# Preparing q and k of a head two heads ahead instead of one, with a third buffer for the transposed operands

## The chip, the cores and the metric

The kernel runs on one core of one Trainium2 chip. Its time is the device time of one launch in microseconds (us). Before the change the median of three runs is 1237.27 us (1229.78, 1237.27 and 1239.12).

## The reference: what is computed

Eight batches of eight heads, 576 positions, 64 columns a head. Attention with a bias from a running sum, then a gated feed-forward layer (FFN) on the 4608 x 512 result:

```
scores = q @ k.T / 8 + min(-(cum[i] - cum[j]), 0)      cum = cumsum(max(s, 0))
scores = where(j > i, -1e9, scores)
attn   = exp(scores - rowmax);  attn /= rowsum + 1e-9
x      = heads side by side of (attn @ v)               4608 x 512
out    = (sigmoid(x @ w_gate) * (x @ w_val)) @ w_out    d_ff = 1536
```

## The kernel before

**The arithmetic.** From head 8 on, float32 operands are split into a high and a low float16 part, and a product is made of several float16 matmuls. For q and k this takes four steps, in `split_qk` and `swap_k`. ScalarE (ACT) writes the high parts of q and k (L370, L372), VectorE (DVE) the low parts (L371, L373), into a tile `t16` of 96 x 12 x 2 x 64. A transposing DMA (L375) issued by SyncE (SP) turns that into `T[i][:, 0:2]`, with the columns of a head down the partitions. Two plain DMAs (L380, L381), also from SP, then write into `T[i][:, 2]` a copy of k's part in which the upper and the lower 64 partitions have changed places. SP issues L380 only once the transposition has landed.

**The scores.** A head has 576 rows in five row tiles (64 rows, then four times 128), worked from the last, t = 4, to the first. For each, `s_part` makes the scores on TensorE (PE) in two matmuls into the same bank: L420 with `T[i][:, 0]`, which needs the transposition alone, and L421 with `T[i][:, 2]`, which needs the two swapping DMAs. Row tile 4 is done in two pieces of 288 columns, so a head has six L420 and six L421. The banks are three ("s", "s", "x"). DVE adds the bias row and takes the row minimum (`max_part`, L445), which frees the bank; POOL masks the bias row (L435); ACT makes the exponential (L448).

**The weights and the output of attention.** `p_part` splits the exponentials (ACT L452, DVE L453), and SP transposes them by DMA (L456, tile `pt`, two a head). `av_part` multiplies them with v on PE (L468 to L470) two heads later.

**The FFN.** A unit (`ffn_in`, L615) is 24 or more matmuls of one group of 256 tokens and one of twelve columns of d_ff into a bank pair `gv`, of which there are two. ACT takes the tanh (L620), DVE the product (L622), which frees the pair. ACT and DVE split the product (L630, L631), and `ffn_out` multiplies with `w_out` (L645).

**What sets the order.** One loop over ticks, five ticks a head (`NTL = 5`), emits a piece of everything: the scores of one row tile, masks and minima of the tile before, the output of an earlier head, the preparation of a later head at fixed ticks, and so many FFN units that a batch's units are spread over the ticks of the next batch. A scheduler takes this emission order as the priority and arranges each engine's instructions with its own estimates of when operands will be there. At run time each engine works off its own list strictly in order and waits where something is missing. Instructions inside `pin(...)` keep the order of the program among themselves.

**The stages.** Heads 0 to 7 use another form (`n_prep`, `n_s`). From tick 90 (head 18, `NOFF + 3`) the space of `t2big`, used before for the first FFN units, becomes free: `more_room` takes a second buffer for `t16` (`qk16`) and one for the loaded q and k (`qk32`) out of it. In profiles and orders those two appear under the name `t2f`. Up to there they have one buffer each. `T` has two buffers of a pool throughout, so `T[i]` is written over `T[i-2]`.

**When q and k are prepared, from head 18 on.** Heads go in pairs p = i // 2, with j = i % 2; all times are ticks t of head i. In an even head (j = 0) the other head of the pair is split at t = 1 and swapped at t = 3. In an odd head (j = 1) the next pair is squared at t = 0 (ACT L340 and a reduction on POOL, for a power of two that scales it), scaled at t = 1 (DVE L348 to L358), the first head of it is split at t = 2 and swapped at t = 4. Its first scores are emitted at the tick that follows.

Of the kernel before, what the change touches and what calls it, by code (L numbers as in the profile page):

```python
# [7 lines left out]
F16 = mybir.dt.float16  # L8
# [8 lines left out]
P = 128  # L17
# [6 lines left out]
def tile_attention_then_gated_ffn(  # L24
# [12 lines left out]
    B, H, S, D = q.shape  # L37
# [166 lines left out]

    def more_room():
        c = 0
        for name, n in (("qk16", QC * 2 * D), ("qk32", 4 * QC * D)):
            spare[name] = t2big[:, c : c + n]
            c += n

# [150 lines left out]
    def split_qk(i):  # L361
        p, j = divmod(i, 2)
        sc = qkc[p][0]
        if spare and i % 2:
            t16 = spare["qk16"][:QP].bitcast(F16).rearrange("p (a c l d) -> p a c l d", a=2, l=2, d=D)
        else:
            t16 = wp.tile([QP, 2, QC, 2, D], F16, tag="qk16", name=f"qk16_{i}", bufs=1)
        q_ = qk32[p][:, 0, j]
        k_ = qk32[p][:, 1, j]
        pin(nc.scalar.activation(t16[:, 1, :, 0], q_, AF.Copy, scale=sc[:QP, 0:1]))  # L370
        nc.vector.scalar_tensor_tensor(t16[:, 1, :, 1], q_, sc[:QP, 0:1], t16[:, 1, :, 0], ALU.mult, ALU.subtract)  # L371
        nc.scalar.activation(t16[:, 0, :, 0], k_, AF.Copy, scale=sc[:QP, 1:2])  # L372
        nc.vector.scalar_tensor_tensor(t16[:, 0, :, 1], k_, sc[:QP, 1:2], t16[:, 0, :, 0], ALU.mult, ALU.subtract)  # L373
        T[i] = wp.tile([P, 3, S], F16, tag="T", name=f"T{i}", bufs=2)
        nc.sync.dma_start_transpose(  # L375
            T[i][:, 0:2].rearrange("p a (c n) -> p (a c) n", n=QP),
            t16.rearrange("p a c l d -> p (a c l d)"))
# [302 lines left out]

    NE, NOFF = 44, 87
    FPT = 1.5
    WLA = 3
    nticks = NTL * NH
    for n in range(nticks + 12):
        if n == NOFF + 3:
# [36 lines left out]

        if t == 1 and NN <= i - 2 < NH:
            with first(NE <= n < NOFF):
                av_part(i - 2, 1)
                av_part(i - 2, 0)
                x_part(i - 2)
            if i % 2 == 1:
                split_x((i - 2) // 2)  # L730

        if i < NH:
            p, j = divmod(i, 2)
            b, h = divmod(i, H)
            if t == 0 and i + 1 < NH:
                load_crow(i + 1)
            if t == (2 if spare else 0) and i + 1 < NH:
                spread_crow(i + 1)
            if i + 2 < NN:
                if j == 0 and t == 1:  # L740
                    n_load(p + 1)
                    load_v(p + 1)
                if j == 1 and t == 2:
                    with first():
                        n_prep(p + 1)
            elif j == 0 and i + 2 < NH:
                if t == 2:
                    if p + 1 not in qk32:
                        load_qk(p + 1)
                    load_v(p + 1)  # L750
                if t == 4 and not spare:
                    qk_square(p + 1)
            if NN <= i and j == 0:
                if t == 0:
                    split_v(p)
                if t == 1:
                    split_qk(i + 1)
            if NN - 1 <= i and j == 1 and i + 1 < NH:
                late = 1 if spare else 0
                if t == 0 and p + 1 not in qkc:  # L760
                    qk_square(p + 1)
                if t == late:
                    qk_scale(p + 1)
                if t == 1 + late:
                    split_qk(i + 1)
                if t == 3 and spare and i + 3 < NH:
                    load_qk(p + 2)
            if t == (3 + j if spare else 3) and NN - 1 <= i and i + 1 < NH:
                swap_k(i + 1)
            if b == 0:  # L770
                if 1 <= n < 1 + vch:
                    v_square(0, n - 1)
                if n == 1 + vch:
                    v_scale(0)
            if b + 1 < B:
                if t == 2 and 1 <= h < 1 + vch:
                    v_square(b + 1, h - 1)
                if t == 4 and 1 <= h < 1 + vch:
                    v_square_sum(b + 1, h - 1)
                if t == 1 and h == 6:  # L780
                    v_scale(b + 1)
            while n < NE and wnext["step"] < min(2 + n // 8, 6):
                weight_step()

        if n >= NE and state["u"] < 2 * NF:
            fdone = min(NF, int((n - NE + 1) * FPT))
            while state["u"] < 2 * fdone:
                f = state["u"]
                if f < NF and f % WLA == 0:
                    while wnext["step"] < f + WLA:  # L790
                        weight_step()
                    inverse_weights(0, slice(f, f + WLA))
                    ffn_scale(0, slice(f, f + WLA))
                while f >= NF and wnext["step"] < min(f + NF + WLA, len(wsteps)):
                    weight_step()
                emit_unit()
            if state["u"] == 2 * NF:
                hidden_scale()
                while state["o"] < 2 * NF:
                    emit_out()  # L800
                late_slots()
        if (n - 30) % (NTL * H) == 0 and n >= 30 + NTL * H:
            ffn_scale((n - 30) // (NTL * H))
        m = n - (9 if n > 2 * NTL * H + 30 else 7)
        b = m // (NTL * H) if m >= 0 else 0
        if b >= 1:
            r = m - b * NTL * H + 1
            done = min(NT, b * S) // GT * NF if b < B else len(units)
            prev = min(NT, (b - 1) * S) // GT * NF
            want = prev + (done - prev) * r // (NTL * H)  # L810
            while state["u"] < min(want, len(units)):
                emit_unit()
# [32 lines left out]
```

## Time and profile before

| | |
|---|---|
| median of three runs | 1237.27 us |
| the profiled execution: its own time / its span | 1237.8 us / 1236.0 us |
| mean granted clock of PE | 0.971 |
| PE busy | 1121.7 us, 91% |
| DVE / ACT / POOL busy | 785.8 us (64%) / 747.1 us (60%) / 302.9 us (25%) |
| scores of heads 8 to 63 on PE, lines L420 and L421 | 111.9 to 1055.5 us of the span |

A group's row gives the line, the engine, the operation, output and inputs, the number of instructions, then busy time, the mean duration of one in ns and the idle time of the engine just before them with what ended it. A row of waits reads: engine, tile and line that waited, what it waited for, the total in us, how many times, the longest. In a timeline each row starts with the start and the duration in us; a bracket at the end gives the idle time before it and what ended it. `SPq` is SyncE issuing a DMA: its duration is the issuing, not the transfer. A row of windows gives for each engine the busy time and the instructions in it, then the granted clock of PE, the share of the DMA engines that is busy and what they moved. After 1055 us there is only the FFN of the last batch.

### The profile page before, as it was taken

The page shows a single profiled execution, that of the slowest core. Times are in us where ns is not written, and L with a number is a line of the kernel's source. Part 1 is how long each engine was busy: PE and PEld are TensorE (multiplying, and loading weights), DVE is VectorE, ACT ScalarE, POOL GpSimd, SP SyncE. Part 2 cuts the span into 40 slices and gives each one's busy share as a digit, 9 for nine tenths or more (in the row PEclk, how much of TensorE's full clock was granted, in tenths as well). Part 3 has the DMA queues.
Part 4 walks back from the last instruction along what each step waited for, and adds up shares of the span by engine and source line. Part 5 has one row for each costly group of instructions (what it writes and reads, how often), then busy time and mean ns, then how long its engine had stood idle before and what let it go on. Part 6 is the DMA issues. An engine that isn't in the chain of part 4 may idle for free.

```text
span 1236.0 us, 30675 instructions
## 1 busy us (share of the span) xinstructions
PE 1121.7 (91%) x11924; PEld 870.4 (70%) x11924; DVE 785.8 (64%) x2194; ACT 747.1 (60%) x1505; POOL 302.9 (25%) x605
## 2 busy tenths in 40 slices
PE   6787789899998899889999989998899899999997
PEld 5575568567776777577777766777777777787774
DVE  6899898767776677556656667765677677322221
ACT  6998786766666666455655656665576666333221
POOL 5544343222132222221212122322232311000000
PEclk9888899999999899899999999999999999999999
DMA  9665897967779777975546576677777755200000
GB/s 276 196 191 120 202 200 153 164 145 148 143 141 153 120 159 144 135 141 92 120 82 138 118 151 138 128 135 148 132 150 144 130 105 122 54 19 7 12 18 18
DMA packets 464176, 157.51 MB, mean 127 GB/s; under 512 B 438495, under 2 KB 457951, under 8 KB 464030
## 3 DMA queue, kind: packets, MB, share of 16 engines
q1 hardware_dynamic: 446302, 119.89, 52.5%
q0 software_dynamic: 5440, 18.88, 5.0%
q10 hardware_dynamic: 12288, 16.78, 4.3%
q8 instruction: 93, 1.52, 0.6%
q14 instruction: 53, 0.43, 0.1%
HBM read 56.92 MB, written 9.58 MB: 54 GB/s over the span
## 4 chain that ended last, share of the span: by engine, by line
PE 38%; issue 22%; DMA 16%; DVE 10%; ACT 6%; SPq 3%; POOL 2%; ACTq 0%; POOLq 0%; DVEq 0%
PE gv L615 20%; PE o L645 10%; DMA T<-T 8%; DMA T<-qk 6%; PE s L421 3%; DVE e L445 2%; PE s L420 2%; SPq L456 1%; SPq L380 1%; DVE p L453 1%; PE av L470 1%; PE av L468 1%; PE av L469 1%; ACT p L452 1%; ACT w L276 1%
## 5 line engine op out<-in xcount | busy, mean ns | idle before, releaser
L615 PE MATMUL gv<-x,w 128*128 128x256 f16 (+3 forms) x6912 | 635.0, 248 | 4.0 <-DVE t2f L622 4.0
L615 PEld LDWEIGHTS <-w 128*128 128x128 f16 x6912 | 541.5, 99 | 72.3 <-issue 5.8
L645 PE MATMUL o<-w2all,h 128*128 128x512 f16 x1296 | 320.0, 383 | 0.0
L435 POOL TENSOR_SCALAR_AFFINE_SELECT rl<-rl 128x64 f32<-128x64 f32 (+1 forms) x280 | 131.3, 471 | 491.1 <-DVE em L445 394.0
L620 ACT ACTIVATE th<-gv,scb 128x256 f32<-128x256 f32 (+3 forms) x288 | 111.5, 413 | 216.6 <-PE gv L615 215.4
L448 ACT ACTIVATE e<-e,em 128x576 f32<-128x576 f32 x280 | 153.8, 555 | 112.9 <-DVE em L445 111.7
L445 DVE CUSTOM_DVE_ANT_0 e<-s,rl,qkcf 128x288 f32<-128x288 f32 x280 | 136.1, 486 | 110.9 <-PE s L421 99.0
L645 PEld LDWEIGHTS <-h 128*128 128x128 f16 x1296 | 124.1, 99 | 106.7 <-issue 3.8
L622 DVE SCALAR_TENSOR_TENSOR t<-th,gv 128x256 f32<-128x256 f32 x192 | 80.2, 418 | 162.5 <-ACT th L620 161.7
L453 DVE SCALAR_TENSOR_TENSOR p<-e,p 128x1152 f16<-128x1152 f32 x112 | 129.6, 1157 | 39.5 <-ACT p L452 39.4
L630 ACT ACTIVATE h<-t,hsc 128x256 f16<-128x256 f32 x192 | 96.9, 505 | 75.7 <-DVE t L622 75.6
L631 DVE SCALAR_TENSOR_TENSOR h<-t,hsc,h 128x256 f16<-128x256 f32 x192 | 93.5, 487 | 53.6 <-ACT h L630 53.0
L421 PE MATMUL s<-T 128*128 128x288 f16 x336 | 81.2, 288 | 48.1 <-DMA T<-T 48.1
L452 ACT ACTIVATE p<-e 128x1152 f16<-128x1152 f32 x112 | 111.4, 994 | 1.2
L420 PE MATMUL s<-T 128*128 128x288 f16 x336 | 82.4, 280 | 24.4 <-DMA T<-qk 19.5
L468 PE MATMUL av<-v,pt 128*128 128x65 f16 x840 | 88.8, 193 | 4.3 <-DMA pt<-p 4.1
L469 PE MATMUL av<-v,pt 128*128 128x64 f16 x840 | 88.6, 193 | 0.0
L470 PE MATMUL av<-v,pt 128*128 128x65 f16 x840 | 88.4, 195 | 0.0
L468 PEld LDWEIGHTS <-pt 128*128 128x128 f16 x840 | 77.9, 98 | 12.2 <-DMA pt<-p 5.5
L469 PEld LDWEIGHTS <-pt 128*128 128x128 f16 x840 | 77.7, 97 | 7.0 <-issue 0.2
L421 PEld LDWEIGHTS <-T 128*128 128x128 f16 x336 | 30.7, 100 | 71.7 <-DMA T<-T 53.3
L470 PEld LDWEIGHTS <-pt 128*128 128x128 f16 x840 | 77.7, 97 | 2.4 <-issue 0.2
(165 smaller groups left out, 1228.4 us busy)
## 6 DMA issues: line engine op xcount, KB each, us to landing
vsq<-in_v_dram POOLq DMA_DIRECT2D x32, 288.0 KB, 4.5
out_dram<-osb POOLq DMA_DIRECT2D x36, 256.0 KB, 2.6
v<-in_v_dram SPq DMA_DIRECT2D x64, 128.0 KB
T<-T SPq DMA_DIRECT2D x112, 72.0 KB
ws<-in_moe_w_out_dram ACTq DMA_DIRECT2D x12, 512.0 KB
qk<-in_q_dram SPq DMA_DIRECT2D x17, 288.0 KB
qk<-in_k_dram SPq DMA_DIRECT2D x17, 288.0 KB
w2all<-in_moe_w_gate_dram ACTq DMA_DIRECT2D x7, 512.0 KB
```

The source lines that it names most:

```text
L421: nc.tensor.matmul(ps[:, : b_ - a], lhs, T[i][:, 2, a:b_], start=False, stop=True)
L435: nc.gpsimd.affine_select(rl[i][:, q0:w], rl[i][:, q0:w], pattern=[[-1, m]], compare_op=ALU.is_ge, fill=-MASKED if i < NN else MASKED, bas ...
L445: nc.vector.tensor_tensor_reduce(e_t[t][:, a:b_], ps[:, : b_ - a], rl[i][:, a:b_], c, init, ALU.add, ALU.min, acc)
L448: nc.scalar.activation(e_t[t][:, :w], e_t[t][:, :w], AF.Exp, bias=init, scale=-1.0)
L452: nc.scalar.activation(p_s[h_][:, 0], e_s[h_], AF.Copy, scale=PSCALE)
L453: nc.vector.scalar_tensor_tensor(p_s[h_][:, 1], e_s[h_], PSCALE, p_s[h_][:, 0], ALU.mult, ALU.subtract)
L468: nc.tensor.matmul(AV[i][:, t], hi, v_[:, D : 2 * D + 1], start=kb == 0, stop=False)
L469: nc.tensor.matmul(AV[i][:, t, 0:D], hi, v_[:, 0:D], start=False, stop=False)
L470: nc.tensor.matmul(AV[i][:, t], lo, v_[:, D : 2 * D + 1], start=False, stop=kb == t)
L615: nc.tensor.matmul(ps[:, gv, a:e], w1[f][:, cc, gv, wl], x_of(b, cc)[:, xl, c0 + a : c0 + e], start=(c == 0), stop=(c == 3 * NC - 1))
L620: nc.scalar.activation(th[:, a:e], ps[:, 0, a:e], AF.Tanh, scale=scb[b][:, f : f + 1])
L645: nc.tensor.matmul(ps[:m], h[:, hl, tt * P : tt * P + m], w2[f][:, wl], start=(f == 0 and c == 0), stop=(f == NF - 1 and c == 2))
```

## The change

From tick 90 the preparation runs two heads ahead. In an even head i the next pair is squared at t = 0, scaled at t = 1, its first head i + 2 is split at t = 2 and swapped at t = 4. In an odd head i, head i + 2, the second of that pair, is split at t = 1 and swapped at t = 3. `load_qk` moves with it: in an odd head, at t = 3, it loads pair p + 3 instead of p + 2. Since three heads' transposed operands are now alive, `T` gets a third buffer out of `t2big`, which every third head (i % 3 == 2) takes; the others share the two of the pool. `T[i]` is thus written over `T[i-3]`. Heads 18 to 20 are a passage: head 19 still prepares head 20, and splits head 21 as well at t = 4. What is computed, and how many instructions of each kind, stays the same. `EARLY = 18` names the head; `NTL * EARLY` is 90 as `NOFF + 3` was.

```diff
     def more_room():
         c = 0
-        for name, n in (("qk16", QC * 2 * D), ("qk32", 4 * QC * D)):
+        for name, n in (("qk16", QC * 2 * D), ("qk32", 4 * QC * D), ("T", 3 * S // 2)):
             spare[name] = t2big[:, c : c + n]
...
-        T[i] = wp.tile([P, 3, S], F16, tag="T", name=f"T{i}", bufs=2)
+        if spare and i % 3 == 2:
+            T[i] = spare["T"].bitcast(F16).rearrange("p (a n) -> p a n", a=3)
+        else:
+            T[i] = wp.tile([P, 3, S], F16, tag="T", name=f"T{i}", bufs=2)
...
+            elif i <= EARLY + 1:
+                if j == 0:
+                    if t == 1:
+                        split_qk(i + 1)
+                    if t == 3:
+                        swap_k(i + 1)
+                        load_qk(p + 2)
+                else:
...
+                    if t == 2:
+                        split_qk(i + 1)
+                    if t == 4:
+                        swap_k(i + 1)
+                        split_qk(i + 2)
+                        load_qk(p + 3)
             elif j == 0 and i + 2 < NH:
+                if t == 0:
+                    if i == EARLY + 2:
+                        swap_k(i + 1)
+                    qk_square(p + 1)
+                if t == 1:
+                    qk_scale(p + 1)
                 if t == 2:
-                    if p + 1 not in qk32:
-                        load_qk(p + 1)
-                    load_v(p + 1)
...
+                    split_qk(i + 2)
+                if t == 4:
+                    swap_k(i + 2)
+            elif j == 1 and i + 2 < NH:
                 if t == 1:
-                    split_qk(i + 1)
...
-                if t == 1 + late:
-                    split_qk(i + 1)
-                if t == 3 and spare and i + 3 < NH:
-                    load_qk(p + 2)
-            if t == (3 + j if spare else 3) and NN - 1 <= i and i + 1 < NH:
-                swap_k(i + 1)
+                    split_qk(i + 2)
+                if t == 3:
+                    swap_k(i + 2)
+                    if i + 6 < NH:
+                        load_qk(p + 3)
```

How this moves instructions, at two places.

First PE, at the start of head 27. `T_6358` is the transposed operand of head 27, `s_4` and `s_3` are banks for its row tiles 4 and 3. Before, the two L420 of row tile 4 stand together, and the first L421 stands much further on:

```order
L420 LDWEIGHTS T_6358
L420 MATMUL s_4_0_6536<-T_6358 128x288
L420 LDWEIGHTS T_6358
L420 MATMUL s_4_288_6539<-T_6358 128x288
L645 LDWEIGHTS h_0_6279
L645 MATMUL o_0_6613<-w2all,h_0_6279 128x512
```

```order
L615 LDWEIGHTS w_5_71
L615 MATMUL gv_5_6799<-x_2799,w_5_71 128x128
L421 LDWEIGHTS T_6358
L421 MATMUL s_4_0_6536<-T_6358 128x288
L421 LDWEIGHTS T_6358
L421 MATMUL s_4_288_6539<-T_6358 128x288
L421 LDWEIGHTS T_6358
L421 MATMUL s_3_0_6621<-T_6358 128x448
```

Now PE's list has the same head, whose operand is `T_6094`, as follows (lines are three further down, L423 and L424 for L420 and L421); `t2f` is here the operand of head 26, in the third buffer:

```order
L423 LDWEIGHTS t2f
L423 MATMUL s_0_0_6548<-t2f 128x64
L424 LDWEIGHTS t2f
L424 MATMUL s_0_0_6548<-t2f 128x64
L423 LDWEIGHTS T_6094
L423 MATMUL s_4_0_6562<-T_6094 128x288
L424 LDWEIGHTS T_6094
L424 MATMUL s_4_0_6562<-T_6094 128x288
L423 LDWEIGHTS T_6094
L423 MATMUL s_4_288_6565<-T_6094 128x288
L424 LDWEIGHTS T_6094
L424 MATMUL s_4_288_6565<-T_6094 128x288
```

Between the first L420 and the first L421 of head 27 there stood 115 other matmuls (56 of the FFN's L615, 12 of L645, 45 of an earlier head's output, two more L420); now the two of a piece stand side by side, straight behind the last piece of head 26.

Second SP's list around the same head. Before, the transposition of head 27's operand (`T_6358`), then a `pt` of head 26, then the swap:

```order
L375 DMA_TRANSPOSE T_6358<-t2f 128x12x96
L330 DMA t2f<-in_q_dram 96x12x64
L456 DMA_TRANSPOSE pt_26_6445<-p_1_82 128x18x128
L380 DMA T_6358<-T_6358 64x576
L381 DMA T_6358<-T_6358 64x576
L386 DMA cr_6888<-cum_d 1x576
L456 DMA_TRANSPOSE pt_26_6626<-p_0_81 128x12x128
```

Now the same head's (`T_6094`) comes one head earlier, beside the `pt` of head 25 (L378 for L375, L383 and L384 for L380 and L381, L459 for L456):

```order
L459 DMA_TRANSPOSE pt_25_6152<-p_1_82 128x18x128
L491 DMA_TRANSPOSE x_131<-x_11_6086 128x10x128
L378 DMA_TRANSPOSE T_6094<-t2f 128x12x96
L330 DMA t2f<-in_q_dram 96x12x64
L389 DMA cr_6574<-cum_d 1x576
L383 DMA T_6094<-T_6094 64x576
L384 DMA T_6094<-T_6094 64x576
L459 DMA_TRANSPOSE pt_25_6306<-p_0_81 128x12x128
L459 DMA_TRANSPOSE pt_26_6471<-p_1_82 128x18x128
```

Both DMAs of the preparation have moved by one head against the `pt` transpositions; no `pt` stands between the transposition and its swap any more at this place.

More of the change, by code (lines that the diff above doesn't have):

```diff
@@ L682, in tile_attention_then_gated_ffn @@
     FPT = 1.5
+    EARLY = 18
     WLA = 3
@@ L685, in tile_attention_then_gated_ffn @@
     for n in range(nticks + 12):
-        if n == NOFF + 3:
+        if n == NTL * EARLY:
             more_room()
@@ L745, in tile_attention_then_gated_ffn @@
                         n_prep(p + 1)
-            elif j == 0 and i + 2 < NH:
-                if t == 2:
-                    if p + 1 not in qk32:
-                        load_qk(p + 1)
-                    load_v(p + 1)
[L751 to L755, printed above, removed]
-                if t == 1:
-                    split_qk(i + 1)
[L758 to L763, printed above, removed]
-                if t == 1 + late:
-                    split_qk(i + 1)
-                if t == 3 and spare and i + 3 < NH:
-                    load_qk(p + 2)
@@ L768, in tile_attention_then_gated_ffn @@
-            if t == (3 + j if spare else 3) and NN - 1 <= i and i + 1 < NH:
-                swap_k(i + 1)
+            elif j == 0 and t == 2 and i + 2 < NH:
+                if p + 1 not in qk32:
+                    load_qk(p + 1)
+                load_v(p + 1)
+            if NN <= i and j == 0 and t == 0:
+                split_v(p)
+            if not spare:
+                if j == 0 and t == 4 and i + 2 >= NN:
+                    qk_square(p + 1)
+                if NN <= i and j == 0 and t == 1:
+                    split_qk(i + 1)
+                if NN - 1 <= i and j == 1:
+                    if t == 0:
+                        qk_scale(p + 1)
+                    if t == 1:
+                        split_qk(i + 1)
+                if t == 3 and NN - 1 <= i:
+                    swap_k(i + 1)
+            elif i <= EARLY + 1:
+                if j == 0:
+                    if t == 1:
+                        split_qk(i + 1)
+                    if t == 3:
+                        swap_k(i + 1)
+                        load_qk(p + 2)
+                else:
+                    if t == 0:
+                        qk_square(p + 1)
+                    if t == 1:
+                        qk_scale(p + 1)
+                    if t == 2:
+                        split_qk(i + 1)
+                    if t == 4:
+                        swap_k(i + 1)
+                        split_qk(i + 2)
+                        load_qk(p + 3)
+            elif j == 0 and i + 2 < NH:
+                if t == 0:
+                    if i == EARLY + 2:
+                        swap_k(i + 1)
+                    qk_square(p + 1)
+                if t == 1:
+                    qk_scale(p + 1)
+                if t == 2:
+                    split_qk(i + 2)
+                if t == 4:
+                    swap_k(i + 2)
+            elif j == 1 and i + 2 < NH:
+                if t == 1:
+                    split_qk(i + 2)
[3 more added lines that the diff above has]
+                        load_qk(p + 3)
```

## The prediction

> **What bounds the kernel now.** The page comes first, with the busy time of the engines:
>
> ```profile
> span 1236.0 us, 30675 instructions
> PE 1121.7 (91%) x11924; PEld 870.4 (70%) x11924; DVE 785.8 (64%) x2194; ACT 747.1 (60%) x1505; POOL 302.9 (25%) x605
> ```
>
> PE is the engine to follow; the other three have a third of the span or more to spare. An engine that works 91% can only get faster where it waits, so the next view is the waits of PE. I look at the stretch from 310 us, just ahead of the first scores of head 21 (the first head that the change prepares earlier), to 1060 us, behind the last scores:
>
> ```profile
> PE s L421 <- DMA T<-T: 41.6, 23, 5.8
> PE s L420 <- DMA T<-qk: 11.9, 12, 2.7
> PE s L420 <- DVE em L445: 0.5, 1, 0.5
> ```
>
> This is all that PE waits for in 750 us: 41.6 us until the swap of T has landed, 11.9 us until the transposition has, and 0.5 us for DVE. There is no wait for a `gv` pair and none for `pt`. The same query over all engines says who waits for whom beside it:
>
> ```profile
> ACT th L620 <- PE gv L615: 112.0, 63, 8.5
> DVE e L445 <- PE s L421: 84.5, 70, 5.9
> ```
>
> ACT and DVE stand behind PE, not PE behind them. So in this stretch the kernel goes as fast as PE's list, and PE's list stops at T alone.
>
> Why is T late? The timeline of SP at the second-longest stop, head 27, and what PE shows there:
>
> ```profile
> 405.81 2.05 SPq L375 DMA_TRANSPOSE T<-t2f  x1
> ...
> 408.69 4.36 SPq L456 DMA_TRANSPOSE pt<-p  x1
> ...
> 409.28 0.42 PE L420 MATMUL s<-T 128*128 128x288 f16 x2
> ...
> 413.14 0.77 SPq L380 DMA_DIRECT2D T<-T  x1
> 413.95 0.59 SPq L381 DMA_DIRECT2D T<-T  x1
> ...
> 420.77 1.04 PE L421 MATMUL s<-T 128*128 128x288 f16 x3 [3.80 <-DMA T<-T]
> ```
>
> The transposition is issued at 405.81; SP then spends 4.36 us issuing a `pt` transposition, the swap follows at 413.14 and 413.95, and PE goes on at 420.77, when it has landed. From issue to the last landing it takes 15.0 us. The longest stop of all, head 33, has the same shape:
>
> ```profile
> 503.89 1.28 SPq L375 DMA_TRANSPOSE T<-t2f  x1
> ...
> 521.04 0.66 PE L421 MATMUL s<-T 128*128 128x288 f16 x2 [5.79 <-DMA T<-T]
> ```
>
> That is 17.2 us from issue to use.
>
> **A second price of the stops: the clock.** The granted clock of PE falls to 0.50 in five stretches after 310 us. I cut each to the part in which PE was working again:
>
> ```profile
> 420.80:426.40 5.60, 5.60 (x46) 4.97 (x46) 3.31 (x12) 0.77 (x1) 1.98 (x3) 0.50 0.65 132
> 521.00:525.40 4.40, 4.36 (x15) 2.22 (x16) 2.58 (x8) 1.98 (x4) 1.42 (x3) 0.50 1.09 245
> 556.10:559.50 3.40, 3.40 (x23) 1.74 (x21) 0.71 (x3) 1.84 (x4) 1.13 (x2) 0.50 0.00 0
> 772.00:778.00 6.00, 6.00 (x34) 4.22 (x34) 3.50 (x11) 3.06 (x4) 2.28 (x4) 0.50 0.28 54
> 856.50:859.90 3.40, 3.40 (x41) 3.00 (x39) 2.89 (x9) 1.49 (x2) 1.43 (x4) 0.50 0.05 10
> ```
>
> Together 5.60 + 4.36 + 3.40 + 6.00 + 3.40 = 22.8 us of PE work at half the clock, or 11.4 us lost. Two begin at the stops of 3.80 and 5.79 us shown above; the other three at these:
>
> ```profile
> 554.77 0.42 PE L421 MATMUL s<-T 128*128 128x288 f16 x2 [3.10 <-DMA T<-T]
> 771.97 1.01 PE L421 MATMUL s<-T 128*128 128x288 f16 x3 [2.48 <-DMA T<-T]
> 856.11 0.71 PE L421 MATMUL s<-T 128*128 128x288 f16 x3 [3.18 <-DMA T<-T]
> ```
>
> **The change part by part.**
>
> *The preparation one head earlier.* From head 21 on, each split and each swap stands five ticks earlier than before, at otherwise the same distance from one another (split at t = 1 or 2, swap two ticks later). What five ticks are worth is read where T hardly stops PE, heads 28 to 32:
>
> ```profile
> 433.92 0.61 PE L420 MATMUL s<-T 128*128 128x288 f16 x3 [1.37 <-DMA T<-qk]
> 493.83 0.42 PE L420 MATMUL s<-T 128*128 128x288 f16 x2 [0.63 <-DMA T<-qk]
> 434.00:494.00 60.00, 59.05 (x724) 46.93 (x725) 44.22 (x130) 40.60 (x81) 15.68 (x33) 1.00 0.74 149
> ```
>
> Four heads in 59.9 us, 15.0 us a head. Head 27's first L420 ran at 409.28, 3.5 us after the issue of its transposition. With one head more there are some 3.5 + 15.0 = 18.5 us for a chain that took 15.0 us, and about the same for head 33's 17.2 us. So even the two worst still just fit, without counting that the swap no longer stands behind a `pt` there, and all shorter ones fit well. I take both rows of waits as gone: 41.6 + 11.9 = 53.5 us. Heads 19 and 20, ahead of 310 us, keep theirs.
>
> *The clock.* All five half-clock stretches after 310 us begin at stops that disappear: 11.4 us. The Trainium skill, "TensorE: Matmul & The Clock Gate", section "Part 1: The HAM clock gate", lets the clock fall after an idle window of about 3.4 us; by that only the stops of 3.80 and 5.79 us would cost clock, and by estimate (5.60 + 4.36) / 2 = 5.0 us would come back instead of 11.4. The trace disagrees as far as the length goes: three stops of 2.48 to 3.18 us were followed by half clock too. The sum uses the rows.
>
> *The work itself.* The instructions are the same in number and kind, so ACT, DVE and POOL do per head what they did. They get less time for it: the stretch above shows DVE with 44.22 us and ACT with 40.60 us in 60, at a PE that worked 59.05 us of them. That is the pace to come: 15.0 us a head less the 0.95 us of idle time in four heads is 14.8 us, where DVE is at 75%. This work stays hidden behind PE. If the cover were gone (DVE later than PE), its price is in the next paragraph.
>
> *What is late next.* PE's list changes: the six pieces of a head no longer have L420 and L421 apart, and the first pieces of a head stand straight behind the last piece of the head before. That asks DVE to free banks sooner. Bounds from rows: the 0.5 us in 750 us above, and the earlier stage, 100 to 290 us, where the order was another and the engines fuller:
>
> ```profile
> PE av L468 <- DMA pt<-p: 4.1, 3, 1.4
> PE s L420 <- DVE em L445: 4.1, 4, 1.5
> PE gv L615 <- DVE t2f L622: 4.0, 6, 1.0
> ```
>
> 12.2 us in 190 us, which over 740 us would be 47.5 us. A gain from this is excluded, since the bank wait is already 0.5 us. The stretch of heads 28 to 32, the same stage with 0.95 us of idle time in 60 us and that for T, is much nearer: I take 5 us, for the new order and the passage at heads 20 to 22.
>
> *SP's list.* The preparation moves past one head's `pt` transpositions, as many as before stand in the queue. `pt` has room: the second one of head 30, and the first use of either on PE:
>
> ```profile
> 482.01 2.09 SPq L456 DMA_TRANSPOSE pt<-p  x1
> ...
> 492.13 0.19 PE L468 MATMUL av<-v,pt 128*128 128x65 f16 x1
> ```
>
> 8.0 us lie between the end of the issue and PE. It is the shortest that I found after 310 us. A swap landed 6.8 us after its issue in the busiest place (413.95 to 420.77), so it holds there by about one us; elsewhere by more. Cost taken: 0.
>
> *The third buffer.* It lies in space that is free by then. T[i] is written over T[i-3] during head i-2, when T[i-3]'s last score is behind; before it was T[i-2] during head i-1, the same distance. No new wait: 0.
>
> *The tail.* From the last scores on there is no T and PE is full:
>
> ```profile
> 1060.00:1230.00 170.00, 167.48 (x1614) 128.07 (x1610) 40.01 (x90) 48.13 (x104) 4.36 (x8) 1.00 0.05 16
> ```
>
> Nothing changes there, and time won earlier brings its start forward in full.
>
> *The sum.* The profiled execution took 1237.8 us, 0.5 us above the median 1237.27. 1237.8 - 53.5 - 11.4 + 5 = 1177.9, and less 0.5 it is 1177.4 as a median; I say 1178.
>
> **The rivals.**
>
> *A new wait takes half or all of what the early stage shows.* DVE frees banks or `gv` pairs too late in the tighter order, or `pt` lands too late. For it speaks that ACT and DVE are planned by estimates, and that the stops gave them 53.5 us to catch up; against it that heads 28 to 32 had no such stops and no such waits. At the full rate 1237.3 - 64.9 + 47.5 = 1220, at half of it 1196. Chance 0.14.
>
> *T does not come earlier.* The splits stand on ACT's and DVE's lists and the transposition in SP's behind `pt`; if they only wait longer there (for the load of q and k, or for PE to be through with the buffer), nothing is won: 1237. For it: SP waits for landings often. Against it: the order shows the transposition and the swap a head earlier on SP, with the instructions that feed them. Chance 0.05.
>
> *SP's queue becomes the pace, and the kernel slower.* SP issues a swap only when its transposition has landed, and everything behind it stands:
>
> ```profile
> SPq L380 <- DMA T<-qk: 22.2, 12, 3.1
> ```
>
> Now swap and transposition often stand with no `pt` between, which could make nearly every swap such a wait. At most that is 3.1 us for each `pt` behind it; it decides from the point where `pt`'s room, some 1 to 2 us in the busy stretches, is used up. Two a head, 6.2 less 2.0 us, stop PE for 4.2 us where both are hit, half of that on average: 43 heads x 2.1 = 90 us, and the clock losses stay: 1237.3 - 53.5 + 90 = 1274. Against it: the wait stands in 12 of the heads already, and PE does not wait for `pt` once after 310 us. Chance 0.04.
>
> *My forecast*, the stops gone and little new, 1172 to 1190: chance 0.77.
>
> **How the numbers follow.** The likeliest case gives 1178. The range reaches below it by the 5 us of new waits not coming and the runs' own spread of a few us (1229.78 to 1239.12 before): 1170. Above, it takes in the first rival up to three quarters: 1210. One per cent, about what a measurement of this kernel can tell from no change, is 12.4 us, so faster means below 1225: forecast and first rival, 0.91, less a little for the latter going beyond its bound: 0.90. Within one per cent: 0.06. Slower: 0.04.
>
> **What would show it.** In the waits of PE after the first scores of head 21, both rows on T should be below 3 us in all; the clock should be 1.00 from there to the last matmul, the mean near 0.98; PE busy, in us, smaller by about 11. A row `gv L615 <- DVE` or `s <- DVE em` above 15 us shows the first rival; `av L468 <- DMA pt` the third; rows on T of unchanged size the second. The forecast is wrong if PE's idle time after 310 us stays above 25 us, whoever is named.

## The result and the profile after

The changed kernel takes 1177.37 us (median of four runs, 1168.54 to 1182.52) against 1238.19 us (four runs, 1229.78 to 1242.22): ratio 0.951, 95% interval 0.9426 to 0.9593. In a second comparison, six runs on another occasion, it took 1173.03 us (1167.70 to 1175.30), ratio 0.9488 (0.9446 to 0.9530). 1178 was forecast. The profiled execution of the first took 1181.64 us, that of the second 1171.78 us. Here and below, executions more than 1.5% above the fastest of the same kernel count as slow and are left out of the medians of the kernels tried and of the ratios.

The page after has PE at 94% of a shorter span:

```profile
span 1179.8 us, 30668 instructions
PE 1110.7 (94%) x11924; PEld 867.9 (74%) x11924; DVE 785.0 (67%) x2194; ACT 758.5 (64%) x1505; POOL 306.9 (26%) x605
```

All that PE waits for between 310 and 1060 us (lines after stand three or more further down: L423 and L424 are the two score matmuls, L618 the FFN's):

```profile
PE gv L618 <- DMA x<-x: 2.4, 3, 1.3
PE s L424 <- DMA t2f<-t2f: 0.5, 1, 0.5
```

The 53.5 us on T have become 0.5 us. What is next late is neither a bank nor a `gv` pair nor `pt`, but `x`: the first FFN units of a batch wait for the transposition of its last pair of heads. The same stretch as windows, before and then after, with PE's busy time first and the granted clock third from the end:

```profile
310.00:1060.00 750.00, 695.92 (x7965) 543.95 (x7963) 494.25 (x1382) 461.21 (x916) 176.75 (x365) 0.98 0.70 132
```

```profile
310.00:1060.00 750.00, 747.04 (x8851) 592.54 (x8848) 517.13 (x1445) 495.01 (x968) 184.39 (x372) 1.00 0.71 136
```

PE works 747 of 750 us, at full clock throughout. Head 27, the example of the prediction, in the timeline of SP after, and then its first scores on PE:

```profile
397.21 1.32 SPq L378 DMA_TRANSPOSE T<-t2f  x1
...
402.35 0.49 SPq L383 DMA_DIRECT2D T<-T  x1
402.89 0.59 SPq L384 DMA_DIRECT2D T<-T  x1
403.58 1.98 SPq L459 DMA_TRANSPOSE pt<-p  x1
```

```profile
411.20 0.29 PE L423 MATMUL s<-T 128*128 128x288 f16 x1
411.32 0.29 PE L424 MATMUL s<-T 128*128 128x288 f16 x1
```

The swap is issued 5.1 us after the transposition (7.3 us before the change), with the `pt` behind it instead of ahead of it, and 9.0 us before PE uses it; nothing stops.

SP's own waits between 310 and 1060 us show a second thing that the change took away. Before, then after (the chosen rows are those of the transposition of q and k waiting for the low parts of the split):

```profile
SPq L375 <- DVE t2f L371: 39.6, 21, 6.6
...
SPq L375 <- DVE qk L371: 18.1, 8, 6.4
```

```profile
SPq L378 <- DVE t2f L373: 2.9, 2, 1.7
...
SPq L378 <- DVE qk L371: 1.0, 1, 1.0
```

Before, SP stood 39.6 + 18.1 = 57.7 us at that transposition because the split was not done, with everything behind it in its list standing too: in the median of the 43 heads from 21 on, it issued the transposition 0.06 us after the last low part was ready. Now it does so 2.6 us after. How long SP stands does not by itself decide the time, though, as experiment 5 shows. And one wait of SP grew with the change, that of the swap for its own transposition, from 22.2 us in 12 places (shown in the prediction) to 63.5 us in 41:

```profile
SPq L383 <- DMA T<-qk: 25.6, 13, 5.2
...
SPq L383 <- DMA T<-t2f: 14.8, 14, 2.3
...
SPq L383 <- DMA t2f<-qk: 13.4, 7, 2.5
SPq L383 <- DMA t2f<-t2f: 9.7, 7, 2.8
```

**An account of eleven profiles.** The code up to tick 90 is the same in all kernels below, so I count from the first score of head 18 to the last matmul. Idle is the sum of PE's idle times above 50 ns, with their number; half is the time at a granted clock of 0.50 in which PE worked; the rest is the length less the idle time and less half of "half". The kernels but the first and the last two are the experiments, told below.

| kernel | first score of head 18 at | length | idle (stops) | half | rest |
|---|---|---|---|---|---|
| before | 271.5 | 956.0 | 56.4 (40) | 22.8 | 888.2 |
| third buffer alone | 269.3 | 952.7 | 51.1 (38) | 27.1 | 888.0 |
| swap two ticks earlier alone | 272.7 | 952.3 | 51.7 (41) | 25.4 | 887.9 |
| after, late swap | 269.3 | 916.8 | 27.4 (21) | 8.0 | 885.4 |
| early split, later DMAs | 278.7 | 905.7 | 18.9 (19) | 2.8 | 885.4 |
| two ticks of lead | 279.3 | 912.2 | 20.8 (13) | 15.6 | 883.6 |
| three ticks of lead | 279.3 | 902.7 | 15.4 (14) | 6.8 | 883.9 |
| two ticks, swap at once | 278.8 | 902.5 | 14.5 (6) | 11.6 | 882.2 |
| after with two buffers | 269.7 | 891.2 | 6.4 (6) | 4.9 | 882.4 |
| after | 284.2 | 887.0 | 4.5 (6) | 0.0 | 882.5 |
| after, second profile | 270.7 | 890.7 | 8.2 (6) | 0.0 | 882.5 |

The rest is nearly a constant, so idle time and half clock carry nearly all differences. What is left follows the number of stops: (888.1 - 882.4) / (40 - 6) = 0.17 us a stop. From the first row to "after" the length falls by 69.0 us: 51.9 idle, 11.4 clock, 5.7 rest.

### The profile page after: what moved, and what is told of

Read it like the earlier page. It is cut to its first block, busy times and chain, and to the rows that moved or that the text cites. A ratio compares the mean times of both kernels' runs of the same rounds, so it can differ in the third digit from the quotient of the medians.

```text
span 1179.8 us, 30668 instructions
## 1 busy us (share of the span) xinstructions
PE 1110.7 (94%) x11924; PEld 867.9 (74%) x11924; DVE 785.0 (67%) x2194; ACT 758.5 (64%) x1505; POOL 306.9 (26%) x605
## 4 chain that ended last, share of the span: by engine, by line
PE 59%; issue 20%; DMA 8%; DVE 5%; ACT 4%; POOL 2%; SPq 0%; ACTq 0%; POOLq 0%; DVEq 0%
PE gv L618 30%; PE o L648 16%; PE s L424 3%; PE s L423 3%; DMA pt<-p 2%; PE av L471 2%; PE av L473 2%; PE av L472 2%; DMA x<-x 1%; DMA qk<-in_q_dram 1%; DMA T<-qk 1%; PE na_ps L566 1%; DVE e L448 1%; PE s L537 1%; DMA T<-T 1%
## 5 line engine op out<-in xcount | busy, mean ns | idle before, releaser
L618 PE MATMUL gv<-x,w 128*128 128x256 f16 (+3 forms) x6912 | 616.7, 247 | 7.2 <-DVE t2f L625 4.7
L618 PEld LDWEIGHTS <-w 128*128 128x128 f16 x6912 | 538.2, 98 | 67.8 <-issue 8.7
L438 POOL TENSOR_SCALAR_AFFINE_SELECT rl<-rl 128x64 f32<-128x64 f32 (+1 forms) x280 | 128.8, 460 | 425.4 <-DVE em L448 373.0
L448 DVE CUSTOM_DVE_ANT_0 e<-s,rl,qkcf 128x288 f32<-128x288 f32 x280 | 134.7, 487 | 48.2 <-PE s L424 30.6
L456 DVE SCALAR_TENSOR_TENSOR p<-e,p 128x1152 f16<-128x1152 f32 x112 | 130.7, 1167 | 30.9 <-ACT p L455 30.1
L471 PE MATMUL av<-v,pt 128*128 128x65 f16 x840 | 85.6, 193 | 12.2 <-DMA pt<-p 12.2
L472 PE MATMUL av<-v,pt 128*128 128x64 f16 x840 | 85.3, 193 | 0.0
L473 PE MATMUL av<-v,pt 128*128 128x65 f16 x840 | 85.3, 195 | 0.0
L423 PE MATMUL s<-T 128*128 128x288 f16 (+2 forms) x246 | 65.4, 285 | 12.8 <-DMA T<-qk 8.5
L656 POOL DMA_DIRECT2D out_dram<-osb x36 | 20.3, 564 | 216.2 <-ACT osb L655 214.2
L392 POOL PARTITION_BROADCAST cr<-cr x63 | 66.7, 1064 | 16.7 <-DMA cr<-cum_d 12.5
```

What stands on the lines that cost most here:

```text
L423: nc.tensor.matmul(ps[:, : b_ - a], lhs, T[i][:, 0, a:b_], start=True, stop=False)
L438: nc.gpsimd.affine_select(rl[i][:, q0:w], rl[i][:, q0:w], pattern=[[-1, m]], compare_op=ALU.is_ge, fill=-MASKED if i < NN else MASKED, bas ...
L448: nc.vector.tensor_tensor_reduce(e_t[t][:, a:b_], ps[:, : b_ - a], rl[i][:, a:b_], c, init, ALU.add, ALU.min, acc)
L456: nc.vector.scalar_tensor_tensor(p_s[h_][:, 1], e_s[h_], PSCALE, p_s[h_][:, 0], ALU.mult, ALU.subtract)
L471: nc.tensor.matmul(AV[i][:, t], hi, v_[:, D : 2 * D + 1], start=kb == 0, stop=False)
L472: nc.tensor.matmul(AV[i][:, t, 0:D], hi, v_[:, 0:D], start=False, stop=False)
```

## The experiments

All are compared with the kernel before, run beside them; experiments 1 to 4 share a chip, so do 5, 6 and 10, and so do 7, 8, 9 and 11.

**1. The third buffer alone.** The kernel before with the two edits on the buffer and nothing else:

```diff
-        T[i] = wp.tile([P, 3, S], F16, tag="T", name=f"T{i}", bufs=2)
+        if spare and i % 3 == 2:
+            T[i] = spare["T"].bitcast(F16).rearrange("p (a n) -> p a n", a=3)
+        else:
+            T[i] = wp.tile([P, 3, S], F16, tag="T", name=f"T{i}", bufs=2)
```

> The third buffer alone: the kernel before, in which from tick 90 every third head's T lies in the space of t2big, with the preparation at its old ticks, one head ahead. Theory (lead time): PE's stops come from the chain split, transposition, swap being longer than the two to four ticks it has, so a further buffer changes nothing: 1230 to 1246 us, the two rows of PE waiting for T after 310 us together 45 to 60 us, half-clock stretches after 310 us still there. Rival (buffer): the transposition of T[i] stood on SP until PE had read T[i-2]; with the buffer it goes out earlier and most stops vanish: below 1200 us, rows below 15 us.

Measured: 1234.39 us, ratio 0.9995 (0.9955 to 1.0035). The rows on T after 310 us add up to 48.2 us. The buffer alone does nothing; the rival falls.

For most of the next ones split, transposition and swap were emitted by a list of ticks, each with its own lead over the old tick; with five, five and five its ticks are those of the changed kernel.

**2. Early split, transposition and swap at the old ticks.**

```diff
-    LEAD_SPLIT, LEAD_TURN, LEAD_SWAP = 5, 5, 5
+    LEAD_SPLIT, LEAD_TURN, LEAD_SWAP = 5, 0, 0
```

> The third buffer, and from head 21 on ACT and DVE square, scale and split q and k one head (five ticks) earlier as in the changed kernel, but the transposition and the swap are issued at the old ticks. Theory (lead time, and it is the DMA part that is long: 15.0 us from issue to landing at head 27): most stops stay, rows on T after 310 us 30 to 55 us, 1210 to 1240 us. Rival (split chain): ACT and DVE splitting late is what holds the transposition back, so an early split is enough: rows below 15 us, 1178 to 1195 us.

Measured: 1190.98 us, ratio 0.9643 (0.9585 to 0.9702); rows on T 16.6 us, all of them the swap's:

```profile
PE s L430 <- DMA T<-T: 14.1, 11, 2.8
PE s L430 <- DMA t2f<-t2f: 2.5, 2, 2.1
```

The time is in the rival's range and the rows are just above its 15 us; the theory's 30 to 55 us are far off. But the kernel did not keep apart what it should. The transposition is not pinned, and once its operands were early the scheduler moved it up by itself: the median from its issue to the L420 that uses it is 15.2 us, 4.2 us before. Only the swap stayed late. So this does not tell a late split from a long DMA part; it tells that the early split brings the early transposition with it.

**3. Two ticks of lead.**

```diff
-    LEAD_SPLIT, LEAD_TURN, LEAD_SWAP = 5, 5, 5
+    LEAD_SPLIT, LEAD_TURN, LEAD_SWAP = 2, 2, 2
```

> The changed kernel with the whole preparation two ticks earlier than before the change instead of five (some 5.9 us of lead instead of 15). Theory (PE's list is made from estimates): the scheduler closes the distance that it had put between L420 and L421 and so spends the two ticks; what stops PE is the difference between real and estimated chain, which stays: rows on T after 310 us 20 to 50 us, 1200 to 1235 us. Rival (any lead above the longest stop, 5.8 us, is enough): rows below 5 us, 1173 to 1185 us.

Measured: 1201.58 us, ratio 0.9721 (0.9665 to 0.9777), in the theory's range. Rows on T:

```profile
PE s L430 <- DMA T<-T: 10.4, 5, 3.2
PE s L430 <- DMA t2f<-t2f: 7.4, 4, 2.9
```

17.8 us, 3.0 of them head 20's, whose preparation this list does not touch: just below the theory's 20 to 50, and not the rival's. A lead of 5.9 us does not remove stops of at most 5.8. That the scheduler's estimates are the reason was a guess; experiments 6 and 7 point to another.

**4. The changed kernel with a late swap.**

```diff
-    LEAD_SPLIT, LEAD_TURN, LEAD_SWAP = 5, 5, 5
+    LEAD_SPLIT, LEAD_TURN, LEAD_SWAP = 5, 5, 0
```

> The changed kernel, split and transposition five ticks earlier, but the two swapping DMAs of each head at the old ticks, two or one before its first scores. Theory: the row of L420 waiting for the transposition is gone (below 2 us, it was 11.9), the row of L421 waiting for the swap stays in good part, since a swap landed 3 to 7 us after its issue: 15 to 45 us, 1195 to 1225 us. Rival (the swap is short once the transposition is done early): both rows below 5 us, 1173 to 1185 us.

Measured: 1196.37 us, ratio 0.9687 (0.9651 to 0.9724). The row of the transposition is gone, the swap's is 20.4 + 5.2 = 25.6 us, as the theory gave. With all else early, the time of the swap alone is worth some 22 to 25 us, by the ratios 0.951 and 0.9488 of the changed kernel, which was measured on other occasions.

**5. The change without its third buffer.** Splitting five ticks earlier, T in two buffers; transposition one tick and swap two ticks earlier than before, as early as two buffers allow.

```diff
-    LEAD_SPLIT, LEAD_TURN, LEAD_SWAP = 5, 5, 5
+    LEAD_SPLIT, LEAD_TURN, LEAD_SWAP = 5, 1, 2
...
-        if spare and i % 3 == 2:
-            T[i] = spare["T"].bitcast(F16).rearrange("p (a n) -> p a n", a=3)
-        else:
-            T[i] = wp.tile([P, 3, S], F16, tag="T", name=f"T{i}", bufs=2)
+        T[i] = wp.tile([P, 3, S], F16, tag="T", name=f"T{i}", bufs=2)
```

> The change without its third buffer: from head 21 on the splitting five ticks earlier as in the changed kernel, T with two buffers, so that a transposition can only go out once the scores of the head two before are done; transposition emitted one tick and swap two ticks earlier than before the change, the earliest that two buffers allow. If the third buffer is needed (theory: the DMA part alone, 6 to 17 us from the issue of a transposition to the L421 that uses it, must fit between the last score of a head and the first of the next but one, 15 us, with SP standing at the transposition until PE lets go): rows of PE waiting for T after 310 us 8 to 30 us, 1185 to 1212 us. If the early splitting is the whole gain and the buffer only a convenience: rows below 4 us, 1173 to 1183 us.

Measured: 1171.62 us, ratio 0.9471 (0.9389 to 0.9554), with hardly a row on T:

```profile
PE gv L621 <- DMA x<-x: 4.9, 4, 4.1
PE s L427 <- DMA T<-T: 0.4, 1, 0.4
```

The third buffer is not needed. With the split ready, the transposition goes out 0.9 us (median) after the start of the last score of the head two before, which releases the buffer, against 14.5 us before the change; from there to the use there are 14.4 us (median), and that suffices. Of the change's two parts the earlier preparation is the whole gain.

SP stands at this transposition as long as ever: all its waits there between 310 and 1060 us add up to 91.3 us (90.4 before the change, 48.5 after it), most of them now for PE:

```profile
SPq L381 <- PE s L427: 68.4, 29, 6.8
```

So it is not SP's standing as such that cost time before, but how late the transposition and the swap came for the scores that use them.

**6. Three ticks of lead.** As experiment 3 with 3, 3, 3.

> The changed kernel with three ticks of lead instead of five (two ticks left 17.8 us of PE waiting for T after 310 us, five leave 0.5). Theory (stops go as the lead passes what the scheduler's estimate falls short of the real chain, 0 to 6 us a head): 2 to 10 us of stops, 1178 to 1192 us. Rival (the stops depend on which DMAs share SP's list at the tick, not on the lead): 15 us or more, 1195 us and above.

Measured: 1192.41 us, ratio 0.9613 (0.9542 to 0.9684); rows on T 6.6 + 6.4 = 13.0 us, 3.1 of them head 20's. That lies between the two forecasts and is only 5 us less than with two ticks, while five ticks leave nothing: the lead in ticks is not the whole measure.

So I sorted the heads from 21 on, with the later experiments 7 and 8 as well, by SP's list: does a `pt` transposition of the head just before stand between the transposition and the swap of this head? The stops are the idle time of PE before the first L420 and L421 of these heads.

| kernel | with such a pt: heads, stops | without: heads, stops |
|---|---|---|
| before | 32, 35.4 us | 11, 18.6 us |
| third buffer alone | 32, 32.1 us | 11, 17.0 us |
| early split, later DMAs | 32, 16.9 us | 11, 0.0 us |
| after, late swap | 33, 25.7 us | 10, 0.0 us |
| two ticks of lead | 20, 14.8 us | 23, 0.0 us |
| three ticks of lead | 21, 10.0 us | 22, 0.0 us |
| two ticks, swap at once | 0 | 43, 0.0 us |
| swap two ticks earlier alone | 9, 6.6 us | 34, 43.3 us |
| after with two buffers | 0 | 43, 0.4 us |
| after | 0 | 43, 0.0 us |

In every kernel with any lead, all stops but one of 0.4 us are in heads of the first kind. Without lead (before, third buffer alone, swap two ticks earlier alone) that is not so; experiment 8 takes this up.

An example of the first kind is head 28 with two ticks of lead, on SP and then on PE:

```profile
415.81 2.22 SPq L384 DMA_TRANSPOSE T<-qk  x1
418.12 1.56 SPq L465 DMA_TRANSPOSE pt<-p  x1
...
424.06 3.10 SPq L465 DMA_TRANSPOSE pt<-p  x1
427.26 1.36 SPq L497 DMA_TRANSPOSE x<-x  x1
428.67 0.58 SPq L389 DMA_DIRECT2D T<-T  x1
```

```profile
433.38 0.30 PE L430 MATMUL s<-T 128*128 128x288 f16 x1 [2.83 <-DMA T<-T]
```

The transposition is out 12 us ahead of head 28's scores, but the swap stands behind the first `pt` of head 27, issued at 424.06, and lands too late.

**7. Two ticks of lead, the swap at the tick of its transposition.** Only the swap differs from experiment 3: it is emitted two ticks earlier and, within its tick, behind the transposition.

```diff
-    LEAD_SPLIT, LEAD_TURN, LEAD_SWAP = 2, 2, 2
+    LEAD_SPLIT, LEAD_TURN, LEAD_SWAP = 2, 2, 4
```

> The kernel of two ticks' lead (17.8 us of PE waiting for T after 310 us), in which alone the swap is emitted two ticks earlier still, at the tick of its own transposition. There all the stops fell on even heads, in which SP's list has a pt transposition of the head just before between transposition and swap; now none has. Theory (what counts is whether a swap stands behind a pt whose exponentials are only just being made): rows on T 0 to 3 us, 1168 to 1184 us, as with five ticks of lead. Rival (the lead in ticks counts): 8 to 18 us, 1187 to 1203 us.

Measured: no stop on T in any head from 21 on (14.8 us in experiment 3), as the theory gave; the 3.9 us below are head 20's, whose preparation is not touched:

```profile
PE gv L624 <- DMA x<-x: 9.0, 4, 3.9
PE s L429 <- DMA t2f<-qk: 3.9, 1, 3.9
```

Head 28 now, on SP:

```profile
414.33 2.04 SPq L384 DMA_TRANSPOSE T<-qk  x1
416.46 1.51 SPq L465 DMA_TRANSPOSE pt<-p  x1
418.51 0.47 SPq L389 DMA_DIRECT2D T<-T  x1
419.02 0.59 SPq L390 DMA_DIRECT2D T<-T  x1
```

The time is another matter: 1188.68 us, ratio 0.9621 (0.9569 to 0.9673), better than 1201.58 but not the 1168 to 1184 forecast; it lies in the rival's range. In the profile the waits for `x` are 9.0 us here (2.4 and 5.9 us in the two profiles of the changed kernel), with 11.6 us of work at half clock behind two of them and head 20's, and the stretch up to tick 90 held a stop of 7.7 us that comes and goes (last section). Why `x` comes later here was not tried.

Here the swap's place and its lead in ticks change together. Experiment 5 separates them in part: its swap is emitted two ticks ahead of the old tick, as in experiment 3, yet no `pt` of the head before stands ahead of it in any of the 43 heads, and 0.4 us of stops is left. Its split is three ticks earlier and its transposition one tick later than in experiment 3, so the two kernels differ in more than the place.

**8. The kernel before with the swap two ticks earlier.** One head ahead, two buffers, one line changed:

```diff
-            if t == (3 + j if spare else 3) and NN - 1 <= i and i + 1 < NH:
+            if t == (1 + j if spare else 3) and NN - 1 <= i and i + 1 < NH:
                 swap_k(i + 1)
```

> The kernel before, one head ahead and with two buffers, in which alone the swap is emitted at the tick of its split, two ticks earlier. SP's list then has a pt of the head just before between transposition and swap in 9 of the 43 heads from 21 on instead of 31. Theory (place on SP's list): of the stops, 53.5 us, those of such heads (32.7 us) go by more than half, those of even heads without a pt between (18.6 us) stay, as they have no lead at all: rows on T 20 to 36 us, 1200 to 1222 us. Rival (one head is simply too short for the chain): rows 40 to 55 us, 1227 to 1245 us.

Measured: 1234.45 us, ratio 0.9980 (0.9941 to 1.0019). Rows on T:

```profile
PE s L421 <- DMA T<-T: 28.9, 24, 2.8
PE s L420 <- DMA T<-qk: 20.3, 13, 3.6
```

49.2 us, the rival's forecast. By heads: the odd ones fell from 24.5 to 6.5 us as the place on the list would have it, but the even ones rose from 29.5 to 43.3 us. Those are split last, in the odd head straight ahead of their scores, and PE, no longer held up at the odd heads, reaches them sooner. That this is why they rose was not tried.

The table above counts a `pt` only where it stands between transposition and swap. Without lead the transposition itself often stands behind it, and the swap with it: in 20 of the 21 even heads both stand behind a `pt` of the head before. Counted by the swap alone, 27 heads of this kernel have such a `pt` ahead of their swap, with 44.7 us of stops, and 16 have none, with 5.1 us; these 16, all odd, had 23.5 us before. By this count all 43 heads are of the first kind before the change and with the third buffer alone, and the kernels with a lead stay as in the table. So the place helps where it is reached, and the even heads cannot reach it as long as they are split so late. The changed kernel gives them both, the earlier split and the place.

**9. The changed kernel again**, to compare the others of its call with:

> The changed kernel once more, on the same chip as the other three, to compare them with: 1170 to 1182 us, rows on T after 310 us below 3 us.

Measured: 1173.03 us, no row on T after 310 us, and `x` alone is left:

```profile
PE gv L618 <- DMA x<-x: 5.9, 4, 3.3
```

**10 and 11. The stage before tick 90, one tick earlier.** There two buffers for T and one for the loaded q and k allow no more than a tick. The loads at t = 2 move to t = 1 with it.

```diff
-                if j == 0 and t == 4 and i + 2 >= NN:
-                    qk_square(p + 1)
-                if NN <= i and j == 0 and t == 1:
+                if j == 0 and t == 3 and i + 2 >= NN:
+                    qk_square(p + 1)
+                if j == 0 and t == 4 and i + 2 >= NN:
+                    qk_scale(p + 1)
+                if NN <= i and j == 0 and t == 0:
                     split_qk(i + 1)
...
-                if t == 3 and NN - 1 <= i:
+                if t == 2 and NN - 1 <= i:
                     swap_k(i + 1)
```

> The changed kernel, and besides in the stage before tick 90, which it leaves as it was, squaring, scaling, splitting and swapping one tick earlier (one tick is all that two buffers of T allow there). In the changed kernel PE waits 10.7 us for T between 100 and 290 us, two stops of 3.7 us among them, each with 6.8 us at half clock behind it. If the accounting by stops and clock holds there as well: 3 to 8 us of the stops go and up to 7 us of clock, 1165 to 1174 us against 1177. If this stage is bound by ACT and DVE (77% and 73% busy), which only have the same work in another order: no change, 1173 to 1182 us.

Measured: 1169.61 us, ratio 0.9452 (0.9405 to 0.9498). The time is in the first forecast's range, but the rows on T between 100 and 290 us, which were to give it, hardly moved (4.9 + 4.8 = 9.7 us). With the swap at t = 1:

> The changed kernel with preparation one tick earlier before tick 90, and the swap there at one tick behind the split instead of two. If the place on SP's list counts in that stage too: T rows between 100 and 290 us below 8 us (10.6 us in the changed kernel), 1160 to 1172 us, 3 to 12 us below the changed kernel beside it. If that stage is bound by ACT and DVE or by chance delays of DMAs: within 3 us of the changed kernel.

Measured: 1176.95 us, ratio 0.9531 (0.9483 to 0.9578), 4 us above the changed kernel beside it instead of 3 to 12 below. The rows on T are 8.2 + 0.2 = 8.4 us in the profile, just above the 8 that were named. Neither is shown to differ from the changed kernel: the intervals of both overlap the two of that kernel.

## Why the prediction was right, and where it was not

**What bounds the kernel: right.** PE's list stopped at T alone, and removing that wait moved the time by what it had cost. The rows it named, 41.6 and 11.9 us, went to 0.5 and 0.

**The sum.** Rows on T: 53.5 forecast, 53.0 gone. Clock: 11.4 forecast, and the work at half clock went from 22.8 us to none from 310 us to the last matmul. New waits: 5 forecast, 2.4 and 5.9 us in two profiles; the size holds, the place does not. I had looked at banks, `gv` pairs and `pt`; it is `x`. The trace of before has no wait for it; that T's stops had given it the time is likely but not shown. One term is missing: 5.7 us of the rest, 0.17 us for each of 34 stops.

The net gain from head 18 on is 69.0 us by the first profile and 65.3 us by the second, where the sum had 53.5 + 11.4 - 5 = 59.9. That the first median still came out within 1 us of the forecast is partly luck: the stretch ahead of head 18, whose code is unchanged, took 12.7 us longer in the first profile, one of the four runs, than in that of before (284.2 against 271.5). The profile of the second comparison, whose median is 1173.0 us, is without it. PE's busy time fell by 11.0 us as forecast, but the mean clock was 0.970 in the first profile, not 0.98, for the same reason; the second has 0.981.

**The preparation one head earlier: right in effect, half wrong in the reason.** The step counted lead against the length of the chain, 18.5 us against 15.0, and set the swap's place behind a `pt` aside. Neither number held at head 27: its transposition is issued 14.0 us before its first score (397.21 to 411.20), which would not have covered the old chain of 15.0. On SP's list only the swap has moved by a whole head against the `pt`, past two of them; the transposition has passed just one, not both as the description of the change says. It sufficed because the chain became shorter: the second swap is issued at 402.89, and by the 2.0 to 3.2 us that eight such swaps of this profile took to land, the chain is some 8 to 9 us by estimate. Experiments 3, 5, 6 and 7 point to the swap's place as what counts: with two or three ticks of lead every remaining stop is in a head whose swap stands behind the `pt` of the head before, and an earlier swap that stands ahead of it removes them all. Experiment 8 shows that without an earlier split only some heads can have that place, and that the time then stays as it was. I also did not read SP's own waits, which showed 57.7 us of standing at the transposition for the split.

**The clock: right, and against the page.** By the estimate from the Trainium skill, "TensorE: Matmul & The Clock Gate", section "Part 1: The HAM clock gate", 5.0 us would have come back instead of 11.4. The account by rows closes with half of all half-clock work, to 0.17 us a stop.

**The third buffer: right that it costs nothing, and more than that.** It is not needed (experiment 5). The prediction took the two parts as one.

**SP's list: right.** `pt` was not once waited for after 310 us. **The tail: right**, PE full to its end.

**The rivals.** No new wait of DVE came (first); T did come earlier (second); SP did not become the pace (third): nearly every swap does now wait for its transposition, as that rival said (63.5 us in 41 places), but PE never waited for the `pt` behind it. SP's list is what decides, in the other direction: the change put the swap ahead of the `pt`.

## What to carry to other kernels

Where the bounding engine stops at operands that another step prepares, the wait row was worth its idle time and the half clock behind it here; both could be read before the change was made. Before buying a buffer for an earlier preparation, look at the issuing queue's order and at what it waits for: here two buffers did as well as three once the operands were split early, and a small DMA queued behind a transposition that waits for the head before kept 14.8 and 10.0 us of stops with two and three ticks of lead. The sum of a queue's own waits is no measure of the loss: it was the same with and without the gain. When the wait is gone, look for the next one, here `x`.

## What the runs showed of the hardware that was not expected

**Half clock after short stops.** In all thirteen profiles, after 290 us, all 10 stops of PE of 3.57 us and more came with a stretch at a granted clock of 0.50, of 3.4 or 6.8 us; of the 32 stops from 2.03 to 3.44 us, 20 did and 12 did not; of the 68 from 1 us to there, 2 did. Each stretch is counted to the longest stop in the 7 us ahead of it.

**A stop costs a little more than its idle time**, 0.17 us by the account above. The traces show why: in dense rows between 310 and 1060 us the next matmul starts 0.163 us (median) before the booked end of the one ahead of it, before and after alike, and a stop is counted only from that end. The end is modelled by the profile, so this is a matter of the booking as much as of the engine.

**A chance delay of some ten us.** In the stretch ahead of tick 90 six of thirteen profiles have one stop of 7.7 to 10.4 us at the `pt` of head 11, the others none above 1.6 us at any `pt`; of the two profiles of the changed kernel one has it and one has not. In the first, SP is 13.6 us in issuing two `pt` transpositions, and PE stands:

```profile
177.09 13.60 SPq L459 DMA_TRANSPOSE pt<-p  x2
190.79 2.35 SPq L378 DMA_TRANSPOSE T<-qk  x1
```

```profile
192.74 0.23 PE L471 MATMUL av<-v,pt 128*128 128x65 f16 x1 [9.30 <-DMA pt<-p]
```

What holds up the DMAs there stays open. It may be a good part of what the runs of one kernel differ by; only one run of each kernel and comparison has a trace, so that is not shown.
